# A pre-norm block with an FFT convolution and a Mish MLP: a DFT table loaded instead of built, one transform dropped for planned SBUF copies, row-tiled shift matmuls, and normalisation interleaved with the MLP

## The chip, the cores and the metric

The kernel runs on one core of a Trainium2 chip. The metric is device time in microseconds (us), taken as the median over repeated executions. Most executions of one kernel agree within a fraction of a per cent. A run is called slow when it lies more than 1.5% above the fastest run of the same kernel. The span of a profile is a little shorter than the time (for the kernel before 316.3 us against 317.99).

Engine names: PE is the matmul engine (PEld its weight loads), DVE is VectorE, ACT is ScalarE, POOL is GpSimd, SP is the engine that issues the bulk of the DMAs here.

## The reference

Sequence 2048, width 640, MLP width 1728, bf16 inputs. Cut to what matters:

```python
x = q
h  = x + A(layernorm(x), k, v, shift_k, ssm_k, ssm_D)
h2 = h + mish(layernorm(h) @ w1 + b1) @ w2

def A(q, k, v, shift_k, ssm_k, ssm_D):
    k_shift = causal 4-tap filter of k along the sequence, per channel
    kv = k_shift * v
    y  = irfft(rfft(kv, 4096) * rfft(ssm_k, 4096))[:2048]   # long convolution
    return q * (y + kv * ssm_D)
```

All inputs are normal with a scale of 0.05 or less, so the convolution branch A is small beside x.

## The kernel before

The Fourier transform is two matmul stages. In stage one, 128-column tables act on 128-row blocks. In stage two, a block table G (128 x 128 for each of 128 frequencies) acts on what stage one left. A spectrum then lies in 128 partitions: real parts in rows 0 to 63, imaginary parts in rows 64 to 127. The complex product of the spectra X (of kv) and KP (of the kernel) needs re*re and im*im, and also re*im and im*re, so one factor must be there a second time with its halves exchanged. The inverse runs in two stages again. Then every one of 16 token tiles goes through a chain: multiply by layernorm(x), add x, statistics, normalise, transpose. The MLP takes the transposed tokens.

The emitter lists operations with dependences and estimated durations; a planner written in Python orders them for each engine by priority. On the chip each engine works through its own queue strictly in that order. Parts that the change touches (cut):

```python
    # G is built on PE from a compact table, and evicted by ACT and DVE
    for dl in range(4):
        for cp in range(4):
            ...
            nc.tensor.matmul(pg[:, c2 * 512:(c2 + 1) * 512], sel_b[:, dl, :], E2["r0b"][:, c * 512:(c + 1) * 512], ...)
            ...
            ev(e, Gv[:, cp * 32:(cp + 1) * 32, :, dl, :], src)

    # stage two; for kv a second, swapped transform gives the exchanged halves
    nc.tensor.matmul(ps2v[:, fl, :], G[:, f1, :], src[:, f1, d0:d1], start=True, stop=True)
    ...
    nc.tensor.matmul(pssv[0:64, fl, :], G[:, f1, 64:128], src[:, f1, d0:d1], start=True, stop=True)
    nc.tensor.matmul(pssv[64:128, fl, :], G[:, f1, 0:64], src[:, f1, d0:d1], start=True, stop=True)

    # products: KP = X * KP (half of them straight from PSUM), P2 = swapped X * KP
    nc.vector.tensor_tensor(P2[:, dsl, fsl], xb_rt.tile[:]..., kp, ALU.mult)
    nc.vector.tensor_tensor(kp, psr, kp, ALU.mult)

    # shift filter: 4 full 128x128 diagonal matmuls for each of 16 tiles and 5 channel blocks
    nc.tensor.matmul(pksv[:, tl, :], lhs, PL["diagm"][:, dc * 4 + j, :], start=(j == 0), stop=(j == 3))

    # the chain: stage by stage over all tokens (priorities 79 to 82), then the MLP (100 and up)
    o_pe  = OP(f"i2pe{t2}", ("pe", 0.62), i1_evs + t2m_ops, ..., prio=80)     # inverse, second stage
    o_wb  = OP(f"wb{t2}", ("dve", _dve1(640)), [o_pe, o_lnx], ..., prio=80)
    o_bn  = OP(f"ln2_{t2}", ("dve", 0.9), [o_h], ..., prio=81)
    o_trpe = OP(f"trpe{t2}", ("pe", 0.35), [o_dr], ..., prio=82)
    UNITS = [256, 512, 512, 512, 256]                                          # MLP columns per unit
```

## Time and profile before

317.99 us median of 5 runs (317.83 to 320.43). Read from the timelines of PE and DVE, the span has three parts.

| part | from, to (us) | what runs |
|---|---|---|
| head | 0 to 156.0 | loads, G, transforms, products, inverse's first stage |
| gap | 156.0 to 181.8 | the chain on DVE; PE mostly waits |
| MLP | 181.8 to 316.3 | matmuls of the MLP, then a short tail |

The page of the kernel before: the span, busy time by engine, and the span in 40 slices (one digit is the busy share of a slice in tenths; PEclk is the granted clock of PE in the same way).

```profile
span 316.3 us, 7715 instructions
PE 269.6 (85%) x3431; PEld 200.7 (63%) x3438; DVE 171.6 (54%) x286; ACT 167.4 (53%) x223; POOL 29.4 (9%) x61
PE   0529999998999676999757598999999999999995
DVE  0546669989897999996399998110121012002202
PEclk9985589999999979999995579999999999999999
```

One slice is 7.9 us. PE starts in the second slice and runs at about half its clock in slices 4 and 5, where it builds G. In slices 20 to 23 PE's digits fall to 5 to 7 while DVE has nines from slice 21 on: that is the gap. The granted clock falls to a half in slices 22 and 23. From slice 24 on PE is full, and from slice 26 on DVE is nearly idle.

The chain of work that ended last, by engine, on the same page, shows that the end hangs on PE (all of it in the MLP's lines):

```profile
PE 39%; DVE 3%; ACT 3%; issue 1%
```

Groups of instructions of the kernel before (line, engine, operation, output <- input, shapes, count | busy us, mean ns of one | idle time of the engine just before them and what ended it):

```profile
L370 PE MATMUL ps_g<-early,sel_b 32*128 32x512 bf16 x32 | 13.8, 625 | 6.1 <-ACT bks L286 6.1
L488 PE MATMUL ps_s2vs<-bvs,G 128*64 128x128 bf16 (+1 forms) x256 | 15.5, 206 | 4.2 <-ACT xb L622 3.4
L622 ACT CAST xb<-ps_s2vs 128x1024 bf16<-128x1024 f32 x20 | 20.2, 1026 | 9.0 <-PE ps_s2vs L489 8.5
L576 DVE TENSOR_TENSOR kvb<-ps_ks,kvin 128x1024 bf16<-128x1024 f32 x10 | 18.7, 1928 | 2.2 <-PE ps_ks L567 2.2
L635 DVE TENSOR_TENSOR KP<-ps_s2v,KP 128x1024 bf16<-128x1024 f32 x10 | 12.2, 1220 | 0.0
L648 DVE TENSOR_TENSOR KP<-xa,KP 128x1024 bf16<-128x1024 bf16 x10 | 7.1, 712 | 0.0
L567 PE MATMUL ps_ks<-diagm,kT 128*128 128x128 bf16 x320 | 18.4, 219 | 0.1
```

In order: building G (32 matmuls, 13.8 us of PE); the swapped transform (15.5 us with its twin line) and its eviction (20.2 us of ACT); the kv multiply, which writes with a stride (1.93 us each); the product from PSUM (1220 ns) beside the same product from SBUF (712 ns); the shift filter (18.4 us).

### The profile page before, as it was taken

How to read it: one execution, taken by the hardware profiler on the slowest of the kernel's cores; microseconds unless marked ns; L12 is line 12 of the kernel's file. 1: busy time of each engine (PE TensorE's matmuls, PEld its weight loads, DVE VectorE, ACT ScalarE, POOL GpSimd, SP SyncE). 2: the span in 40 equal slices, each digit the busy share in tenths (PEclk: the TensorE clock that was granted, in tenths of full speed). 3: DMA queues.
4: the chain of work that ended last, by engine and by line, in shares of the span. 5: the costliest groups of instructions: out<-in, count | busy, mean ns of one | idle time of the engine just before them, and what ended most of it. 6: DMA issues, size and time to landing. Idle time of an engine off the chain costs nothing. (4 is left out here: it accounts for less than half of the span.)

```text
span 316.3 us, 7715 instructions
## 1 busy us (share of the span) xinstructions
PE 269.6 (85%) x3431; PEld 200.7 (63%) x3438; DVE 171.6 (54%) x286; ACT 167.4 (53%) x223; POOL 29.4 (9%) x61
## 2 busy tenths in 40 slices
PE   0529999998999676999757598999999999999995
PEld 0513588898988565889634276654674476457783
DVE  0546669989897999996399998110121012002202
ACT  1427688127949868766945779536105600650250
POOL 6000000000000131004111256000000000000000
PEclk9985589999999979999995579999999999999999
DMA  6998000000004651000194000010010001001101
GB/s 185 247 322 356 4 2 4 3 3 2 2 4 144 257 153 51 4 5 2 16 390 155 0 2 3 0 44 0 23 41 21 2 21 41 23 0 42 43 2 41
DMA packets 8097, 21.05 MB, mean 67 GB/s; under 512 B 864, under 2 KB 4896, under 8 KB 7264
## 3 DMA queue, kind: packets, MB, share of 16 engines
q1 hardware_dynamic: 7840, 20.42, 19.0%
q8 instruction: 27, 0.44, 0.6%
q0 software_dynamic: 224, 0.14, 0.4%
q14 instruction: 6, 0.05, 0.1%
HBM read 17.94 MB, written 2.62 MB: 65 GB/s over the span
## 5 line engine op out<-in xcount | busy, mean ns | idle before, releaser
L854 ACT ACTIVATE ub<-ps_ph,b1s 128x512 bf16<-128x512 f32 (+1 forms) x70 | 42.0, 607 | 71.3 <-PE ps_ph L846 69.8
L879 DVE TENSOR_TENSOR ob<-ps_po,xn 128x640 bf16<-128x640 f32 x16 | 13.2, 825 | 103.0 <-PE ps_po L870 103.0
L846 PE MATMUL ps_ph<-b,wts 128*128 128x512 bf16 (+1 forms) x343 | 63.3, 343 | 2.8 <-ACT b L815 2.2
L870 PE MATMUL ps_po<-wts,ub 128*128 128x320 bf16 x448 | 61.7, 299 | 0.2 <-ACT b L816 0.2
L870 PEld LDWEIGHTS <-ub 128*128 128x128 bf16 x448 | 43.8, 98 | 17.5 <-issue 0.3
L846 PEld LDWEIGHTS <-wts 128*128 128x128 bf16 x350 | 35.1, 100 | 29.9 <-issue 2.7
L471 PEld LDWEIGHTS <-G 128*128 128x128 bf16 x512 | 22.6, 97 | 8.0 <-issue 6.3
L622 ACT CAST xb<-ps_s2vs 128x1024 bf16<-128x1024 f32 x20 | 20.2, 1026 | 9.0 <-PE ps_s2vs L489 8.5
L768 PE MATMUL ps_i<-zb,t2m_b 128*128 128x320 bf16 x64 | 14.5, 382 | 6.8 <-DVE lnx L781 5.7
L775 ACT ACTIVATE lnx<-xn,nmr,r1v 128x640 bf16<-128x640 bf16 x16 | 14.0, 916 | 11.3 <-DVE xn L785 8.4
L576 DVE TENSOR_TENSOR kvb<-ps_ks,kvin 128x1024 bf16<-128x1024 f32 x10 | 18.7, 1928 | 2.2 <-PE ps_ks L567 2.2
L714 PE MATMUL ps_i<-a_b,KP 128*128 128x128 bf16 x160 | 18.4, 219 | 1.2 <-ACT zb L286 1.1
L488 PE MATMUL ps_s2vs<-bvs,G 128*64 128x128 bf16 (+1 forms) x256 | 15.5, 206 | 4.2 <-ACT xb L622 3.4
L370 PE MATMUL ps_g<-early,sel_b 32*128 32x512 bf16 x32 | 13.8, 625 | 6.1 <-ACT bks L286 6.1
L471 PE MATMUL ps_s2v<-bvs,G 128*128 128x128 bf16 (+1 forms) x256 | 14.5, 202 | 4.9 <-DVE KP L635 1.7
L567 PE MATMUL ps_ks<-diagm,kT 128*128 128x128 bf16 x320 | 18.4, 219 | 0.1
L715 PE MATMUL ps_i<-a_b,P 128*128 128x128 bf16 x160 | 18.4, 219 | 0.0
L567 PEld LDWEIGHTS <-kT 128*128 128x128 bf16 x320 | 17.9, 98 | 0.3 <-DVE kT L288 0.3
L429 PE MATMUL ps_k<-ident_b,early 128*128 128x128 bf16 x80 | 7.6, 281 | 11.3 <-DVE early L417 11.3
L715 PEld LDWEIGHTS <-P 128*128 128x128 bf16 x160 | 15.6, 98 | 1.6 <-issue 1.5
L286 ACT CAST zb<-ps_i 128x1024 bf16<-128x1024 f32 x16 | 15.4, 1020 | 1.9 <-PE ps_i L715 1.7
L768 PEld LDWEIGHTS <-t2m_b 128*128 128x128 bf16 x64 | 7.6, 119 | 13.2 <-issue 8.9
(77 smaller groups left out, 453.5 us busy)
## 6 DMA issues: line engine op xcount, KB each, us to landing
early<-in_A_ssm_k_dram SPq DMA_DIRECT2D x5, 512.0 KB, 8.5
kvin<-in_A_k_dram SPq DMA_DIRECT2D x2, 1280.0 KB, 19.7
kvin<-in_A_v_dram SPq DMA_DIRECT2D x2, 1280.0 KB, 22.0
xn<-in_A_q_dram SPq DMA_DIRECT2D x2, 1280.0 KB, 6.9
out_dram<-ob SPq DMA_DIRECT2D x16, 160.0 KB, 1.8
wts<-in_B_w_dram SPq DMA_DIRECT2D x1, 2160.0 KB, 8.0
wts<-in_B_w_dram SPq DMA_DIRECT2D x1, 2080.0 KB, 14.5
t2m_f<-tab_t2m SPq DMA_DIRECT2D x8, 256.0 KB, 2.9
```

The source lines that it names most:

```text
L286: nc.scalar.copy(o, i)
L471: nc.tensor.matmul(ps2v[:, fl, :], G[:, f1, :], src[:, f1, d0:d1], start=True, stop=True)
L488: nc.tensor.matmul(pssv[0:64, fl, :], G[:, f1, 64:128], src[:, f1, d0:d1], start=True, stop=True)
L567: nc.tensor.matmul(pksv[:, tl, :], lhs, PL["diagm"][:, dc * 4 + j, :], start=(j == 0), stop=(j == 3))
L576: nc.vector.tensor_tensor(kvb_rt.tile[:, :, tg * 8:(tg + 1) * 8], pksv.rearrange("p t d -> p d t"), vn[:, tg * 8:(tg + 1) * 8, dc * P:(dc ...
L622: nc.scalar.copy(xb_rt.tile[:].rearrange("p (g f) -> p g f", f=nf), pssr)
L714: nc.tensor.matmul(pzv[:, dgl, :], KP[:, dg, :], a12_b[:, 0, :], start=True, stop=False)
L715: nc.tensor.matmul(pzv[:, dgl, :], P2[:, dg, :], a12_b[:, 1, :], start=False, stop=True)
L768: nc.tensor.matmul(pyv[:, hf, 0:320], PL["t2m_b"][:, t2, ri, :], zb[:, ri, t2, hf * 320:(hf + 1) * 320], start=(ri == 0), stop=(ri == 1))
L846: nc.tensor.matmul(ph[:, 0:w], W["w1s"][:, dc, fc * P:(fc + 1) * P], lnhT[:, dc, c0:c0 + w], start=(dc == 0), stop=(dc == NDC - 1))
L854: nc.scalar.activation(hb_of(u)[:, fc, 0:w], rt.tile[:, 0:w], ACT.Mish, bias=b1s[:, fc:fc + 1], scale=1.0)
L870: nc.tensor.matmul(pov[:, hf2, 0:320], hb[:, fc, tl * P:(tl + 1) * P], W["w2s"][:, fc, hf2 * 320:(hf2 + 1) * 320], start=(fc == 0), stop=( ...
```

## The change

Its intent is to shorten the head and the gap; the MLP's work stays.

1. G comes ready-made from memory by DMA (4 MB), not built on PE.
2. The swapped second transform goes. DMAs copy KP half to half within SBUF into KPS, and both products read SBUF.
3. The shift filter uses 32-row matmuls, four row groups side by side, and its multiply writes pairs of values.
4. Transposes write bf16 into PSUM.
5. The 160 blocks are worked in two channel groups (96 and 64), so that stages overlap.
6. Twelve of 16 tokens' chains go beneath the MLP: priorities by token (CHAIN), smaller first MLP units, PSUM split in two rings, one flat arena of SBUF with hand-placed buffers.

The diff, cut to its core:

```diff
-UNITS = [256, 512, 512, 512, 256]
+UNITS = [128, 128, 256, 512, 512, 512]
+CHAIN = [80, 80.5, 81, 81.5] + [100.3, 100.31, 101.3, 101.31] + [102.3, ...] + [103.3, ...]
...
-            o_pe = OP(f"gpe{dl}_{cp}", ("pe", 0.46), [c_r0], allocs=[rt], uses=[early2], emit=gpe, prio=6)
+        DMA(f"d_G{c}", 1.05e6, (lambda e, c=c: nc.sync.dma_start(G_t()[:, c * 32:(c + 1) * 32, :]..., dram["G"][...])), ...)
...
-                        nc.tensor.matmul(pssv[0:64, fl, :], G[:, f1, 64:128], src[:, f1, d0:d1], start=True, stop=True)
-                        nc.tensor.matmul(pssv[64:128, fl, :], G[:, f1, 0:64], src[:, f1, d0:d1], start=True, stop=True)
+            def emit_swap(e, half=half, grp=grp):
+                d0, d1 = GRP_DG[grp]
+                a, b = (0, 64) if half == 0 else (64, 0)
+                nc.sync.dma_start(KPS_t()[a:a + 64, d0:d1, :].rearrange("p g f -> p (g f)"),
+                                  KP_t()[b:b + 64, d0:d1, :].rearrange("p g f -> p (g f)"))
+            DMA(f"d_swap{grp}_{half}", 64 * nd * 256, None, r=[("KP", grp, ci) for ci in range(len(ch))],
+                w=[("KPS", grp, half)], prio=2, after=[...])
...
+                for i in range(4):
+                    rows = slice(32 * i, 32 * i + 32)
+                    lhs = kt.tile[rows, src, 2:P + 2] if src >= 0 else kt.tile[rows, src + 16, 1:P + 1]
+                    nc.tensor.matmul(outs[i // 2][:, i % 2, src + j0:src + j1, :], lhs, diagm[rows, dc * 4 + j0:dc * 4 + j1, :], ...)
...
+            for tt in (KP_t(), KPS_t()):
+                kp = tt[:, d0:d1, f0:f0 + nf]
+                nc.vector.tensor_tensor(kp, x, kp, ALU.mult)
...
+        pr = CHAIN[t2]
+        o_pe = OP(f"i2pe{t2}", ("pe", 0.57), ..., allocs=[rt], emit=pe, prio=pr)
```

## The prediction

> **What bounds the kernel now.** The time is 317.99 us, the span 316.3. Three parts, from the timelines of PE and DVE. (1) Head, 0 to 156 us: transforms and the inverse's first stage, whose matmuls end at 156. PE first works at 11.3 us; from 23.0 to 36.8 it builds table G: 32 matmuls of 625 ns at half clock. From 40 to 150 us the windows view sums 99 us DVE and 76 us ACT busy: evictions and products, 80% of two engines; PE near 90%. (2) 156 to 182 us: normalisation chain, DVE about 100% busy, PE waiting for it; the clock falls to 0.50. (3) 182 to 313 us: the MLP, PE-bound; the chain of waits is 39% PE, all in the MLP lines (512-column matmul 219 ns apart, 320-column 136 ns).
>
> **What the change does, by traced durations.**
> - G comes ready-made from memory (4.2 MB): removes 13.8 us of PE and 17.6 us of evictions; adds DMA: about 12 MB until v has landed, 34 us at the 356 GB/s seen; hidden, I expect.
> - The swapped second transform goes: 15.5 us of PE, 20 ACT evictions (20.2 us). Instead DMAs copy KP half-to-half (5 MB within SBUF), off the critical path.
> - Products: all from SBUF in bf16. Ten from PSUM at 1.22 us become 0.67. The Trainium skill (VectorE: DVE Perf Modes, "The perf-mode tier table") has tensor_tensor 2x in SBUF, 1x from PSUM; the trace agrees (670, 1220 ns).
> - Shift convolution: 320 full matmuls (57 ns apart, 18.3 us) become 380 with 32 rows on four row groups; with the concurrency that the skill's TensorE: Matmul & The Clock Gate, Part 3 gives (3.07x; no run here shows it yet) I estimate 10 us. Its multiply (1.93 us x10) writes pairs: about 1.3 us.
> - Transposes go to bf16 PSUM: 20 evictions at perhaps 0.7 us on DVE, not 1.2.
> - Two channel groups overlap stages; weights load earlier; twelve of sixteen tokens' chains go beneath the MLP, with PSUM split for it.
>
> **Budget.** Head: evictions and products come to 81 us each on ACT and DVE when balanced; PE needs 83. At 85% use, from about 9 us: the inverse's first stage ends at T = 104 instead of 156 (-52). Then 8 us of chain latency before the MLP instead of 26 (-18). Then PE-bound: MLP 123 us, inverse second stage 8.7, transposes 4.9, less what fits in the gap, plus 2 us of low clock and 3.8 of tail: T + 148, a span of 252.
>
> Nearly all is on the critical path: the MLP follows the head. The MLP itself gains nothing; its 128-column units cost about 1 us.
>
> **Prediction: 255 us, range 240 to 272; faster by over 2%: 0.96, within 2%: 0.03, slower: 0.01.**
>
> **What would show it.** PE's first work at 5 to 8 us; last matmul of the inverse's first stage at 95 to 112; DVE and ACT each 80 to 90% busy until there; first MLP matmul 7 to 11 us later; then PE over 95% busy at full clock; chain of waits over 45% MLP lines.
>
> **What would make it wrong.** Row-group matmuls not running side by side (+8 us). Slow copies within SBUF or a late G, with products or stage two waiting (+5 to 15). bf16 PSUM reads gain nothing on DVE (+5). Four PSUM slots tie the engines in lockstep: use 75% (+12). The first units starve for tokens, DVE having deferred statistics too (+5). Better: DVE and ACT above 90% (-6).

## The result and the profile after

247.12 us median of 9 runs (246.78 to 247.9), against 317.99 before: faster, ratio 0.7774, 95% interval 0.7755 to 0.7794. Ratios here and below are the mean time of one kernel's fast runs over that of the other's fast runs of the same rounds, so not quite the ratio of the medians quoted. The comparison with the reference passed.

The page of the changed kernel, the same lines; one slice is now 6.1 us:

```profile
span 245.9 us, 6840 instructions
PE 219.3 (89%) x3018; PEld 166.4 (68%) x3024; DVE 156.4 (64%) x300; ACT 138.7 (56%) x192; POOL 22.6 (9%) x56
PE   1997998988669989399999999999999999999993
DVE  0889998999997998888998886148721011200121
PEclk9999999999998999959999999999999999999999
```

PE starts in the first slice (at 5.0 us in the timeline), there is one low slice (the 17th) in place of four, and one with a low clock (the 18th) in place of two. DVE works on in slices 18 to 25, beneath the MLP. The chain of waits, by engine and by line, now reaches back into the head:

```profile
PE 62%; DVE 28%; issue 3%; POOL 2%; DMA 2%; ACT 1%; DVEq 0%; POOLq 0%; ACTq 0%
PE banks L761 25%; PE banks L745 21%; DVE arena L639 10%; DVE arena L318 9%; PE banks L438 4%; DVE arena L527 4%; DVE st L598 3%; PE banks L464 2%; PE banks L689 2%; PE banks L726 2%; PE banks L409 2%; DMA consts<-tab_consts 2%; POOL r1v L344 2%; PE banks L516 1%; PE banks L493 1%
```

L761 and L745 are the MLP (46% together); L639, L318 and L527 are products, evictions and the kv multiply on DVE. So the head is bound mostly by DVE.

The windows view gives, for a stretch of time, each engine's busy time (PE, PEld, DVE, ACT, POOL), the clock, the DMA share and GB/s. The first line is the kernel before, 40 us to the end of its head; the second the changed kernel, 40 us to the end of its head:

```profile
40.00:156.00 116.00, 102.37 (x2312) 95.93 (x2307) 100.27 (x132) 82.27 (x87) 9.21 (x12) 0.98 0.13 43
```

```profile
40.00:97.50 57.50, 49.26 (x1234) 45.53 (x1234) 55.41 (x93) 49.73 (x56) 2.54 (x6) 0.97 0.39 144
```

DVE was busy 86% (100.27 / 116) and is now busy 96% (55.41 / 57.5). The groups that answer to those of before, with each shape apart (the changed kernel has no group for building G or for the swapped transform):

```profile
L318 DVE CAST arena<-banks 128x1024 bf16<-128x1024 f32 x24 | 28.6, 1219 | 2.4 <-PE banks L651 1.2 <-PE banks L410 0.9 <-ACT arena L316 0.2
L527 DVE TENSOR_TENSOR arena<-banks,arena 128x512 bf16<-128x512 f32 x20 | 12.3, 684 | 1.0 <-ACT arena L316 0.8
L639 DVE TENSOR_TENSOR arena<-arena 128x1024 bf16<-128x1024 bf16 x16 | 9.7, 688 | 0.0
L318 DVE COPY arena<-banks 128x1024 bf16<-128x1024 bf16 x11 | 7.1, 679 | 6.2 <-PE banks L464 6.0
```

The kv multiply went from 18.7 us to 12.3, a bf16 eviction takes 679 ns where an fp32 one takes 1219, and all products run at the SBUF rate. This is the tier table of the Trainium skill (VectorE: DVE Perf Modes, "The perf-mode tier table"): tensor_tensor at 2x from bf16 SBUF and 1x from PSUM, a copy from PSUM up to 2x; the ratios here are 1220/688 and 1219/679, both about 1.8.

Where the 70 us of span went (times of the last first-stage matmul of the inverse and of the first MLP matmul, from PE's timelines):

| part | before | after | difference |
|---|---|---|---|
| head | 156.0 | 97.4 | -58.6 |
| gap | 25.8 | 9.2 | -16.6 |
| MLP and tail | 134.5 | 139.3 | +4.8 |

Twelve tokens' inverse second stage and transposes now lie inside the MLP part; PE's busy time in it rose from 128.6 to 134.8 us.

**Work that is not done.** The copies of point 2 do not appear in the changed kernel's list of DMA issues; the only entries there are loads and the output. Its DMA total on the page:

```profile
DMA packets 7311, 23.38 MB, mean 95 GB/s; under 512 B 689, under 2 KB 4594, under 8 KB 5874
```

The diff shows why: the third argument of `DMA(f"d_swap...")` is the function that emits the instruction, and it is `None`. `emit_swap` is written and never passed. The planner reserves time for the copies, and nothing is issued. The products then read whatever earlier inputs lie in KPS's place, so half of the complex product is wrong, and the comparison with the reference still passes. Experiments 1 and 2 follow this up.

### The profile page after: what moved, and what is told of

It is laid out like the page before. It is cut to its first block, busy times and chain, and to the rows that moved or that the text cites. A ratio compares the mean times of both kernels' runs of the same rounds, so it can differ in the third digit from the quotient of the medians.

```text
span 245.9 us, 6840 instructions
## 1 busy us (share of the span) xinstructions
PE 219.3 (89%) x3018; PEld 166.4 (68%) x3024; DVE 156.4 (64%) x300; ACT 138.7 (56%) x192; POOL 22.6 (9%) x56
## 4 chain that ended last, share of the span: by engine, by line
PE 62%; DVE 28%; issue 3%; POOL 2%; DMA 2%; ACT 1%; DVEq 0%; POOLq 0%; ACTq 0%
PE banks L761 25%; PE banks L745 21%; DVE arena L639 10%; DVE arena L318 9%; PE banks L438 4%; DVE arena L527 4%; DVE st L598 3%; PE banks L464 2%; PE banks L689 2%; PE banks L726 2%; PE banks L409 2%; DMA consts<-tab_consts 2%; POOL r1v L344 2%; PE banks L516 1%; PE banks L493 1%
## 5 line engine op out<-in xcount | busy, mean ns | idle before, releaser
L316 ACT CAST arena<-banks 128x1024 bf16<-128x1024 f32 (+3 forms) x74 | 67.1, 1003 | 16.5 <-PE banks L410 9.9
L751 ACT ACTIVATE arena<-banks,b1s 128x512 bf16<-128x512 f32 (+2 forms) x84 | 44.1, 548 | 47.2 <-PE banks L745 46.0
L745 PE MATMUL banks<-arena 128*128 128x512 bf16 (+2 forms) x414 | 65.1, 314 | 0.9 <-DVE arena L318 0.6
L761 PE MATMUL banks<-arena 128*128 128x320 bf16 x448 | 62.3, 299 | 0.0
L761 PEld LDWEIGHTS <-arena 128*128 128x128 bf16 x448 | 43.6, 98 | 16.8
L745 PEld LDWEIGHTS <-arena 128*128 128x128 bf16 x420 | 37.3, 102 | 24.7 <-issue 0.7
L318 DVE CAST arena<-banks 128x1024 bf16<-128x1024 f32 (+1 forms) x30 | 35.1, 1206 | 2.7 <-PE banks L651 1.2
L438 PE MATMUL banks<-arena 128*128 128x64 bf16 (+1 forms) x512 | 23.1, 202 | 4.4 <-ACT arena L316 3.1
L438 PEld LDWEIGHTS <-arena 128*128 128x128 bf16 x512 | 20.9, 99 | 6.3 <-issue 5.8
L639 DVE TENSOR_TENSOR arena<-arena 128x960 bf16<-128x960 bf16 (+2 forms) x42 | 24.4, 668 | 0.0
L409 PE MATMUL banks<-consts,arena 128*64 128x128 bf16 x320 | 21.4, 219 | 3.2 <-DVE arena L476 1.2
L410 PE MATMUL banks<-consts,arena 128*64 128x128 bf16 x320 | 21.6, 220 | 0.4 <-issue 0.3
L650 PE MATMUL banks<-consts,arena 128*128 128x128 bf16 x160 | 19.5, 223 | 1.5 <-DVE arena L639 1.3
L409 PEld LDWEIGHTS <-arena 128*64 128x64 bf16 x320 | 18.9, 109 | 2.8 <-DVE arena L476 1.5
L410 PEld LDWEIGHTS <-arena 128*64 128x64 bf16 x320 | 18.5, 110 | 2.9 <-issue 2.8
L651 PE MATMUL banks<-consts,arena 128*128 128x128 bf16 x160 | 19.5, 223 | 0.6 <-DVE arena L639 0.6
L701 DVE TENSOR_TENSOR arena<-banks,arena 128x384 bf16<-128x384 f32 (+1 forms) x32 | 13.7, 469 | 8.9 <-PE banks L689 8.5
L650 PEld LDWEIGHTS <-arena 128*128 128x128 bf16 x160 | 15.9, 100 | 1.4 <-DVE arena L639 1.4
L318 DVE COPY arena<-banks 128x1024 bf16<-128x1024 bf16 (+1 forms) x20 | 11.6, 595 | 8.3 <-PE banks L464 6.0
```

The lines of the kernel that those rows point to most:

```text
L316: nc.scalar.copy(o, i)
L318: nc.vector.tensor_copy(o, i)
L409: nc.tensor.matmul(ps1[0:64, gl, :], lhs, fcfs_b[:, 0, :], start=True, stop=True)
L410: nc.tensor.matmul(ps1[64:128, gl, :], lhs, fcfs_b[:, 1, :], start=True, stop=True)
L438: nc.tensor.matmul(ps2[:, c0:c0 + nd], G_t()[:, f0 + fl, :], src[:, f0 + fl, :], start=True, stop=True)
L639: nc.vector.tensor_tensor(kp, x, kp, ALU.mult)
```

## The experiments

All 12 runs passed the comparison with the reference (which, as x2 shows, says nothing of the convolution branch). Times are medians; the kernel before was run beside each of them, between 315.8 and 320.4 us in all fast runs. The runs were spread over three chips (x9 to x12 on another than the changed kernel), so differences of 1 or 2 us are better judged by the ratios.

| run | base | time (us) | ratio to before (95%) |
|---|---|---|---|
| changed kernel | | 247.12 | 0.7755 to 0.7794 |
| x1_swap_issued | after | 260.84 | 0.8191 to 0.8249 |
| x2_branch_zeroed | after | 247.02 (one run) | |
| x3_before_G_loaded | before | 300.79 | 0.944 to 0.9512 |
| x4_before_token_order | before | 332.6 | 1.0443 to 1.0524 |
| x5_swap_small_pieces | after | 254.39 | 0.796 to 0.8067 |
| x6_swap_early_small | after | 256.37 | 0.8031 to 0.8126 |
| x7_full_shift_matmuls | after | 254.35 | 0.7991 to 0.8058 |
| x8_no_deferral | after | 270.94 | 0.8498 to 0.859 |
| x9_stats_order | after | 249.07 | 0.7831 to 0.7884 |
| x10_swap_split | after | 253.75 | 0.7978 to 0.803 |
| x11_swap_split_2k | after | 252.34 | 0.7892 to 0.7996 |
| x12_stats_after_first | x11 | 255.18 | 0.7998 to 0.8062 |

### x1: issue the copies

```diff
-            DMA(f"d_swap{grp}_{half}", 64 * nd * 256, None, r=[...],
+            DMA(f"d_swap{grp}_{half}", 64 * nd * 256, emit_swap, r=[...],
```

> The changed kernel with the half-to-half copies of KP really issued; as handed over they are only planned (their emit function is never passed on), so the swapped product reads stale data. Theory A (the copies are hidden, as predicted): 246 to 249 us, ratio to the kernel before within 0.774 to 0.783. Theory B (the omission buys time, since the first product starts at 58.4 us and the copies can only begin once the last shift transpose is done near 50 us): the first product starts 3 to 8 us later, time 250 to 256 us. Correct in both.

260.84 us: 13.7 us more than the changed kernel. The copies in the list of DMA issues of x1 (KB each, median us from issue to landing), and the DMA total:

```profile
arena<-arena SPq DMA_DIRECT2D x2, 1536.0 KB, 13.6
arena<-arena SPq DMA_DIRECT2D x2, 1024.0 KB, 9.9
DMA packets 7631, 28.63 MB, mean 111 GB/s; under 512 B 753, under 2 KB 4658, under 8 KB 5938
```

The waits of x1 between 40 and 100 us, of PE and of DVE (total us, times, longest):

```profile
PE banks L516 <- issue: 7.8, 1, 7.8
```

```profile
DVE arena L527 <- PE banks L516: 7.4, 1, 7.4
DVE arena L639 <- DMA arena<-arena: 5.9, 1, 5.9
```

The expectation was missed on both sides: 260.84 us lies above the ranges of theories A and B (the first product starts 7.5 us later, as B had it). The profiled run of x1 was 12.0 us slower than that of the changed kernel (259.72 against 247.72 us). PE's two largest stops without a known wait, 7.8 us (L516) and 3.6 us (L438), and DVE's wait of 5.9 us are the losses on view. They partly overlap, so they don't simply add up.

DVE's wait is plain: the second group's copies go out late (79.9 us) and the products wait for them. PE's stop is odd. It falls in the middle of the shift filter, with "issue" as its cause: the profile shows no semaphore that holds PE. PE's timeline in x1 from 53 to 62 us has just these two rows:

```profile
52.81 0.75 PE L516 MATMUL banks<-diagm,arena 32*128 32x128 bf16 x35
61.36 0.93 PE L516 MATMUL banks<-diagm,arena 32*128 32x128 bf16 x28 [7.81 <-issue]
```

PE does not wait for the copies themselves. The first pair was issued at 47.7 and 48.3 us and landed at 57.5 and 65.7 us (9.9 and 17.4 us, of which the list shows the median, 13.6), so PE starts again 4.3 us before the second has landed. Together they move 3.1 MB in 18.0 us, about 175 GB/s.

### x2: can the comparison see the branch at all?

```diff
-            nc.scalar.activation(lnx.tile, xn_t()[:, t2, :], ACT.Identity, scale=r1v[:, t2:t2 + 1], bias=nmr1[:, t2:t2 + 1])
+            nc.scalar.activation(lnx.tile, xn_t()[:, t2, :], ACT.Identity, scale=0.0)
```

This multiplies the whole convolution branch by zero, so it gives a wrong result.

> Wrong on purpose: the changed kernel with the first normalisation's output set to zero, so the whole convolution branch adds nothing. If the comparison with the reference can see the branch, this run fails it; if the branch is too small beside x (theory: that is why the missing copies pass), it passes. Time unchanged, within 1 us of 247.1.

The comparison passes with no convolution at all, so it cannot vouch for the changed kernel's branch, nor for the branch of any version here that issues the copies. That those versions are right is read from the code (the halves exchange, and the inverse's tables carry the signs), not shown by a run.

### x3: the kernel before, with G loaded

```diff
-    g_ops = []            # 16 x two matmuls and an eviction each
+    g_ops = [DMA(f"d_G{c}", 1.05e6, (lambda e, c=c: nc.sync.dma_start(G[:, c * 32:(c + 1) * 32, :]..., dram["G"][...])),
+                 deps=[d_k[1]], prio=3.5 + 0.01 * c) for c in range(4)]
```

> The kernel before with one part of the change alone: table G comes ready-made from memory instead of being built by 32 matmuls and 16 evictions. Theory A (the 13.8 us of G matmuls at half clock are on the path of the head): 14 to 17 us faster, 301 to 305 us. Rival (DMA for k and v is only delayed by G's 4.2 MB, 11 us, and the shift stage waits for it): less than 8 us faster.

300.79 us, ratio 0.9476: 16 to 17 us come from this alone, as theory A had it (14 to 17). It is more than PE's 13.8 us of building. The table's evictions, 17.6 us on ACT and DVE, went as well, and so did the stretch of half clock in slices 4 and 5: x3's page has none there. The run does not separate the three.

### x4: the kernel before, with the chain ordered by token

```diff
-        o_pe = OP(f"i2pe{t2}", ("pe", 0.62), ..., prio=80)
+        o_pe = OP(f"i2pe{t2}", ("pe", 0.62), ..., prio=79 + 0.05 * t2)
 (and so for every stage of the chain)
```

> The kernel before with one part of the change alone: the normalisation chain is planned token by token (priority by token) instead of stage by stage for all tokens. Theory A (the 26 us between the inverse's first stage and the MLP come from the order, not from the amount of DVE work): first MLP matmul at 168 to 173 us instead of 182, 9 to 13 us faster, 305 to 309 us. Rival (weights landing near 170 us, or the shared PSUM ring, hold it): first MLP matmul after 176 us, under 5 us faster.

332.6 us, slower by 15; both theories missed. The first MLP matmul came at 200.9 us, not earlier. A wait of PE in x4, between 155 and 260 us:

```profile
PE ps_tr L808 <- DVE b L799: 20.8, 11, 3.4
```

The planner had put the transposes of 14 tokens ahead of the first MLP matmul in PE's queue, and each of them now waits for its own token's chain. The order alone does not bring the overlap. In the kernel before, the MLP's activations share memory with the inverse's data, so they cannot start until every token's second stage is done. That deferral needs the new memory layout and the split PSUM of the change is read from the code; no run tests it.

### x5: the copies in pieces of 4 KB a partition

```diff
-                nc.sync.dma_start(KPS_t()[a:a + 64, d0:d1, :]..., KP_t()[b:b + 64, d0:d1, :]...)
+                for g0 in range(d0, d1, 16):
+                    nc.sync.dma_start(KPS_t()[a:a + 64, g0:g0 + 16, :]..., KP_t()[b:b + 64, g0:g0 + 16, :]...)
```

> As x1 (copies issued, same place in the plan), but each copy cut into pieces of 4 KB per partition instead of 24 or 16 KB. In x1 PE sat idle 7.8 us inside the last shift convolution, with no instruction to wait for, until the first pair of copies had landed. Theory A (PE waits for the fetch of its next instructions behind packets of 24 KB): the gap is under 2 us and the time 252 to 256 us. Rival B (PE waits for the copies themselves, or for the bandwidth): the gap stays at 6 to 9 us and the time at 259 to 262 us.

254.39 us: 6.4 us less than x1 with the same bytes, and within theory A's 252 to 256. The waits of x5 between 40 and 100 us, of PE and of DVE (line numbers have moved by one):

```profile
PE banks L493 <- issue: 2.1, 1, 2.1
```

```profile
DVE arena L640 <- DMA arena<-arena: 4.6, 1, 4.6
```

The longest stop of PE without a wait has shrunk from 7.8 to 2.1 us. The wait of the products for the second group's copies stays (4.6 against 5.9).

But piece length is not all that changed. Each piece waits for its own place in memory only, so 5 of the first group's 12 pieces went out from 35.7 us on, 12 us before x1's first copy, and only the other 7 are in flight during the filter. That the same bytes in smaller pieces stop PE less is thus not shown by x5. x10 and x11 below are nearer to it: the same places, 4 KB pieces against 2 KB, and 4.4 against 1.2 us of such stops.

What stops PE without a wait? Instructions come to the engines by DMA too, in packets of 16 KB (queue 8 on the page, taken here for PE's, which has 6042 of the 6840 instructions). The DMA view from 48.8 to 58.5 us, first in the changed kernel, then in x1 (packets, MB, share of the engines' time):

```profile
q8 instruction: 2, 0.03, 1.2%
q14 instruction: 1, 0.01, 0.3%
```

```profile
q1 hardware_dynamic: 106, 2.21, 108.0%
q14 instruction: 1, 0.01, 0.2%
```

In x1 queue 8 has one packet at 47.8 us and its next only at 58.5 us. It landed at 59.9 us, and PE went on 1.5 us later. In the changed kernel the packets start at 47.9, 51.9 and 55.8 us. All eight stops of PE by "issue" of over 1 us in x1, x5, x6, x10 and x11 end 1.3 to 1.6 us after such a packet has landed. So the traces speak for PE waiting for its next instructions. Why the packet comes late is argued: the Trainium skill (DMA: Bandwidth & Descriptors, "Queues, rings and completion order") says that each DMA engine takes turns between queues at packet granularity and drains a whole packet first, which fits a fetch held up among the copies' 24 KB packets. No run here measures these turns.

### x6: the copies early, with a smaller product ring

```diff
-    R_KVB = ring("kvb", 5)
+    R_KVB = ring("kvb", 3)
...
+    swap(0, 0, 80, 0, ("k1pe",))
+    swap(1, 80, 96, 0, ("k1pe", "ktpe"))
+    swap(2, 96, 160, 1, ("k1pe", "ktpe"))
```

The last two kv buffers lie in KPS's place; a ring of three frees it, so the second group's copies need not wait for them.

> Copies issued in 4 KB pieces and earlier: channels 0 to 79 as soon as their KP is complete, the rest after the shift transposes; to free the second group's target, the last two shift products reuse the ring of three buffers instead of lying in it. If what x1 lost is the place of the copies in the plan and their packets, not their bytes: DVE no longer waits for a copy, first product at 58 to 61 us, time 246 to 250 us, and correct with the copies done. If the bytes themselves hurt: 253 us or more.

256.37 us. The expectation of 246 to 250 was missed. DVE no longer waits for copies, but the first product starts at 67.5 us where the changed kernel has it at 58.3. The filter ends 4.0 us later (59.2 against 55.2), with a stop of PE by "issue" of 3.0 us inside it, and the planner then put 64 first-stage matmuls of v between the filter and stage two (59.1 to 63.2 us). How much of the rest is due to the ring of three is not separated.

### x7: the shift filter with full matmuls again

```diff
-                for i in range(4):
-                    rows = slice(32 * i, 32 * i + 32)
-                    nc.tensor.matmul(outs[i // 2][:, i % 2, src + j0:src + j1, :], lhs, diagm[rows, ...], ...)
+                for j in range(4):
+                    nc.tensor.matmul(outs[t2 // 8][:, t2 % 8, :], lhs, diagm[:, dc * 4 + j, :], start=(j == 0), stop=(j == 3))
```

> The changed kernel as handed over with one part undone: the shift convolution by 320 full 128-row matmuls (57 ns apart in the kernel before) instead of 380 on four row groups (1.25 us per 76 in the changed trace). PE's part of it goes from 6.3 to 18.3 us. Theory A (PE is a co-bottleneck of the head): 8 to 12 us slower, 255 to 259 us. Rival B (DVE sets the pace from 38 to 58 us, PE has slack): 1 to 6 us slower, 248 to 253 us.

254.35 us, 7.2 us more than the changed kernel: between the two expectations, and nearer to that of theory A. The cut hides that x7 also builds 128-column diagonals on POOL (4.5 us), cuts the multiply into other pieces (still 685 ns each) and holds stage two's first v transform until the filter is done; the 7.2 us are for all of this together. The window from 40 to 60 us, first in the changed kernel, then in x7:

```profile
40.00:60.00 20.00, 17.64 (x633) 15.66 (x633) 19.83 (x28) 15.43 (x17) 0.26 (x2) 1.00 0.05 11
```

```profile
40.00:60.00 20.00, 20.00 (x438) 19.32 (x436) 15.85 (x21) 9.35 (x10) 0.26 (x2) 1.00 0.02 4
```

With row tiles DVE is full (19.83 of 20) and PE is not; with full matmuls PE is full (20.00) and DVE and ACT starve. So in this stretch the bound moves from PE to DVE. The timeline of the changed kernel gives one channel block of the filter:

```profile
46.45 1.09 PE L516 MATMUL banks<-diagm,arena 32*128 32x32 bf16 x76
```

76 matmuls in 1.09 us, where the kernel before needs 64 at 57 ns, 3.7 us: 3.4 times as fast in this block, the fastest. Over the whole filter PE is busy 6.0 us against 18.4, 3.05 times. The Trainium skill (TensorE: Matmul & The Clock Gate, Part 3, "Measured speedup vs the span model") gives 3.07x for four row tiles at 512 columns; the whole filter agrees, with up to 128 columns.

### x8: the changed kernel without deferral

```diff
-        pr = CHAIN[t2]
+        pr = 80 + 0.001 * t2
...
-                   after=m2.get(u - 2, ()))
+                   after=list(m2.get(u - 2, ())) + [x for x in ops if x.name.startswith("i2pe")])
```

One more line is edited that the cut leaves out: the first normalisation's statistics of tokens 8 to 15 move from priority CHAIN to 58, so ahead of the chain.

> The changed kernel with one part undone: the normalisation chain of all 16 tokens goes stage by stage ahead of the MLP, whose first matmul waits for the last second-stage inverse matmul, as it had to in the kernel before. Theory A (deferring twelve tokens gives the shorter gap): first MLP matmul near 125 to 130 us instead of 106.6, time 257 to 264 us. Rival B (the chain would be hidden anyway): under 251 us.

270.94 us, 23.8 us more. The first MLP matmul comes at 135.4 us, not 106.6. PE's waits in x8 between 95 and 140 us:

```profile
PE banks L689 <- DVE arena L701: 15.7, 12, 9.4
PE banks L726 <- DVE arena L719: 5.9, 2, 5.3
```

The expectation (first MLP matmul at 125 to 130 us, 257 to 264 us) was exceeded. Part of the reason is the line left out of the cut: with the statistics of tokens 8 to 15 ahead of it, the chain starts at 109.39 us, not 101.20. These 8.2 us are not deferral. About 15.6 us of the 23.8, by this estimate, are left for putting chains beneath the MLP, near the 16 to 17 of the loaded table (x3). No run has the one edit without the other.

### x9: does a wait in DVE's queue before the first chain step count?

In the changed kernel DVE stands idle about 1.6 us just ahead of the first chain step, for a small product of tokens 4 to 7 that needs POOL. Its priority was made that of its tokens:

```diff
-        OP(f"ln1f{lo}", ("dve", 0.2), ..., emit=ln1f_emit, prio=45)
+        OP(f"ln1f{lo}", ("dve", 0.2), ..., emit=ln1f_emit, prio=45 if lo == 0 else CHAIN[lo])
```

> The changed kernel as handed over (copies not issued), with one priority altered: the small first-normalisation products of tokens 4 to 15 (one for each four tokens, fed by the GpSimd power) are queued on VectorE where their own tokens' chains stand, no longer ahead of the first chain step, where VectorE's in-order queue stood about 1.6 us waiting for GpSimd. Theory A (from the head to the first MLP matmul VectorE is on the critical path, so a wait taken out of its queue there shows in the time): 1.0 to 2.5 us less than the changed kernel, ratio to the kernel before 0.770 to 0.775. Rival B (something else, the inverse's first stage on PE or ScalarE's evictions, sets the first MLP matmul): within 0.5 us of 247.1, ratio 0.776 to 0.779.

249.07 us: 2 us slower than the changed kernel, so neither theory. The first MLP matmul came at 106.5 us against 106.6. The end of DVE's timeline in the changed kernel, before the first chain step (L701), shows what else stands in that queue (rows left out between; start, length, instruction):

```profile
96.45 0.88 DVE L598 BATCH_NORM_STATS2 st<-arena 128x6 f32<-128x320 bf16 x2
...
99.47 0.83 DVE L598 BATCH_NORM_STATS2 st<-arena 128x6 f32<-128x320 bf16 x2
100.34 0.21 DVE L599 BATCH_NORM_AGGREGATE mv<-st 128x2 f32<-128x12 f32 x1
101.12 0.16 DVE L606 SCALAR_TENSOR_TENSOR nmr<-mv,r1v 128x4 f32<-128x4 f32 x1 [0.57 <-POOL r1v L344]
101.20 0.89 DVE L701 TENSOR_TENSOR arena<-banks,arena 128x384 bf16<-128x384 f32 x2
```

Four tokens' statistics that nobody needs yet are done first, 4 us of them. In x9 they are still there, so the chain started at 101.17 us instead of 101.20. And what was moved took time in DVE's queue later. PE's longest new wait in x9, between 107 and 130 us, a window in which the changed kernel has none:

```profile
PE banks L761 <- DVE arena L701: 1.9, 1, 1.9
```

### x10 and x11: copies issued, each piece as early as its own place allows

```diff
-    swap(0)      # whole group, after all kernel and k transposes
+    swap(0, 0, 80, 0, ("k1pe",))
+    swap(1, 80, 96, 0, ("k1pe", "ktpe"))
+    swap(2, 128, 160, 1, ("k1pe", "ktpe"))
...
+    swap(3, 96, 128, 1, ("k1pe", "ktpe", "s1vpe3", "s1vpe4"))
```

The ring of five stays. x10 has pieces of 4 KB a partition, x11 of 2 KB. Both carry the order of x9.

> Correct version: the copies are issued in 4 KB pieces for each partition, and each piece waits only for what its own place in memory needs (first 80 d-pairs for the kernel transposes, the next 16 also for k's transposes, d-pairs 128 to 159 likewise, and only d-pairs 96 to 127 for the last v transforms), with the product ring kept at five, and with the queue order of x9. Theory A (what was left in x5 was the late second group of copies, 4.6 us of VectorE, and PE's stall beside the first): 247 to 251 us. Rival B (the bytes themselves, while in flight, hold PE's instruction stream whatever their order): 252 to 256 us.

> As x10_swap_split, but in pieces of 2 KB for each partition, twice as many copies. If the stall of PE without a wait depends on the length of the packets in flight, it shrinks again (24 KB packets gave about 8 us, 4 KB about 2 us in its longest gap), and the time is 1 to 2 us below x10. If it depends on the bytes or on the count of packets, the time is that of x10 or up to 3 us more (twice the issues on SyncE).

253.75 us (253.54 to 254.1) and 252.34 us (251.02 to 254.26). x10 fell on the rival's side: DVE waits for no copy there, and yet it is no faster than x5 by more than 1 us. In x10's waits PE loses 2.5 us in the shift filter and 1.9 us in a transpose, both put down to "issue", and the filter's lateness passes on to the kv multiply. Against x9, which has the same queue order and no copies, x10 is 4.7 us slower and x11 3.3; against the changed kernel it is 6.6 and 5.2. Not all of that need be bytes in flight: in x10 and x11 the planner also put 64 first-stage matmuls of v between the filter and stage two. Whether 2 KB pieces help the time is unclear: the two ratios' intervals overlap. PE's longest "issue" wait is 1.2 us in x11, but its profile has this instead, in DVE's waits from 35 to 130 us:

```profile
DVE arena L639 <- DMA arena<-arena: 4.0, 1, 4.0
```

It is the first product, which waits for its copies to land and starts at 63.65 us (58.56 in x9). The profiled run took 254.26 us, and two of the four took 251.0, so this wait need not be in all of them. The order taken over from x9 is in both, and x9 made the version without copies 2 us slower. A version of x11 without it was not run.

### x12: statistics of later tokens only after the first token's chain

```diff
-    for t2 in range(16):          # all first-normalisation statistics here
+    ln1(0, 4)
...
+        if t2 % 4 == 0 and t2:
+            ln1(t2, t2 + 4, [o_dr0])      # o_dr0: token 0's normalisation on DVE
```

> As x11_swap_split_2k (copies issued, 2 KB pieces), with one edge added: the first normalisation's statistics of tokens 4 to 15 (about 1.1 us of VectorE a token, 4.0 us of them between the inverse's first stage and the first chain step in the changed kernel and in x9) may start only after token 0's chain has run on VectorE. Theory A (VectorE's in-order queue between the inverse's first stage and the first MLP matmul is on the critical path, and x9 gained nothing because the statistics still stood in that queue): the first MLP matmul comes 3 to 4.5 us nearer to the last matmul of the inverse's first stage than in x11, and the time is 247.5 to 250 us against 252.3. Rival B (the gap is only moved: the statistics delay the chains of later tokens, and PE stops for them in the MLP by as much): the first MLP matmul comes earlier but the time stays 251 to 254 us. Rival C (PE's inverse second stage or ScalarE's scaling sets the first MLP matmul): neither moves.

255.18 us, against 252.34 for x11. The distance from the inverse's first stage to the first MLP matmul shrank by 2.3 us, from 8.8 us in x11 (103.5 to 112.3) to 6.5 (106.2 to 112.7): as theory A had it in direction, but less than its 3 to 4.5. The time did not shrink, and lies above rival B's 251 to 254 as well. PE pays later, as rival B had it. PE's longest wait in x12, from 107 to 130 us:

```profile
PE banks L767 <- DVE arena L705: 3.5, 1, 3.5
```

Here the profiled run was the slowest of the five (258.23 us), so its order of events is used and not its lengths; that the head ended later there is not explained. The fast runs say that nothing was won; the ratios' intervals of x11 and x12 just miss each other, so x12 is if anything slightly slower.

No version that issues the copies beats the changed kernel, which leaves them out. The fastest that does all of the work is x11 at 252.34 us, 20.6% below the kernel before.

## Why the prediction was right or wrong, point by point

The predicted 255 us was 8 us above the measured 247.12; the range of 240 to 272 held it.

- **What bounds the kernel: right.** Head, gap and MLP were the three parts, and x8 shows that the gap was a part of its own: without deferral it is there again (97.9 to 135.4 us), and of its 23.8 us about 15.6 are left when the 8.2 of the other edited line are taken off.
- **The G table: right.** 13.8 us of PE and 17.6 us of evictions were to go, hidden loads to come. In the kernel before it gave 16 to 17 us (x3), the low clock at its building included, and in the changed kernel PE never waits for G.
- **"Instead DMAs copy KP half-to-half (5 MB within SBUF), off the critical path": this step failed.** The changed kernel does not issue them, which could have been read from the diff: the emit argument is `None`. Issued as written they cost 13.7 us (x1): PE stops for 7.8 and 3.6 us, by the packets' times for its next instructions, and DVE waits 5.9 us for the second group, in part at the same time. The best arrangement tried is still 5.2 us slower than the changed kernel, 3.3 slower than x9, which has its queue order (x11). The list of what could go wrong had "slow copies within SBUF", +5 to 15; the budget had zero.
- **The shift filter: right in kind, mis-sized.** 10 us was written beside the skill's 3.07x, though 18.3 / 3.07 is 6.0. PE was busy 6.0 us with it. Against x7, full matmuls and what goes with them, it is worth 7.2 us of time; there PE, not DVE, is the bound of that stretch.
- **Evictions, products, kv multiply: right.** Predicted 0.7, 0.67 and about 1.3 us; measured 0.679, 0.663 to 0.688, and 2 x 0.684.
- **The use of 85%, which set T = 104: mis-sized.** From 9 us to T, DVE was busy 83.8 us (predicted 81) and ACT 74.6 (81): the work was near the forecast, its use higher. DVE was busy 96% from 40 us to the end of the head, ACT 86% (49.73 / 57.5). T came at 97.4, 6.6 us earlier. This and the missing copies are not independent: the copies, issued, delay T. With them the time is 252 to 261 us, around the predicted 255, so the surplus of 8 us is about what the missing work would cost. That 255 also fits the versions with copies is partly luck: the forecast booked nothing for the copies and too low a use elsewhere, and the two errors offset each other. No run separates them exactly.
- **T + 148: right.** Measured 245.9 - 97.4 = 148.5. The first MLP matmul was to come 7 to 11 us after T and came after 9.2. It was called latency; the timeline under x9 shows other tokens' statistics in DVE's queue there, about 4 us. Putting them later shortens the gap by 2.3 us and gains nothing (x12): PE then stops in the MLP, waiting for DVE (1.9 us in x9, 3.5 in x12).
- **"The MLP follows the head", nearly all on the critical path: right.** The chain of waits has 46% in the MLP's lines (predicted over 45) and 28% on DVE, in the head.

## What to carry to other kernels

Check that a planned operation is really emitted, and count its bytes in the profile; a planner that books time for it and a tolerance that cannot see the branch will both hide its absence. A copy "off the critical path" has two prices beside its bandwidth: the memory it needs free, which sets when it can start, and what it does to others while in flight, so issue it in small pieces as early as each piece's place allows and then look at the engines that have no dependence on it. Where an in-order engine's queue is full, moving work within it can merely move the wait (x9, x12), while taking work out can shorten the stretch (building the table, 16 to 17 us in x3).

## What the Trainium skill lacked or had wrong

- No page names the case that PE stops, waiting for no semaphore, because its next instructions come late while SBUF copies are in flight. It belongs to Runtime: NRT & Kernel Launch, which describes instruction fetch. Here PE stopped for 7.8 us with 24 KB pieces (x1, instruction packets 10.7 us apart, 4 us apart in the changed kernel) and for 2.1 us at the longest with 4 KB pieces (x5). The packet-wise turns between queues that DMA: Bandwidth & Descriptors describes would explain it; no run here shows that they do.
- TensorE: Matmul & The Clock Gate (section "Wait — 56ns, not 53.3ns?") states that start-to-start never drops below about 25 ns however small the matmul. Without the condition that both matmuls use the same rows this does not hold: on different row groups 76 ran in 1.09 us here, 14 ns each. The page's own Part 3, on tiles of rows, has them start closer together; the sentence only lacks the condition.
